# The seven-product tail of an attention and mixing kernel: its two accumulation banks made tiles of their own, its sums and splits put elsewhere

## The chip, the cores and the metric

The kernel runs on one core of a Trainium2 chip. The metric is the device time of one execution in microseconds (us). The engines are TensorE (PE, matrix products; PEld loads its weights), VectorE (DVE), ScalarE (ACT), GpSimd (POOL) and SyncE (SP, which here only starts transfers). Each works through its own list of instructions in order and waits for the others by semaphores. SBUF is the on-chip memory; PSUM holds what PE accumulates, in banks of 512 float32 columns.

## The reference

Three steps follow one another on tensors of 4 batches, 448 tokens and 768 channels.

```python
# 1  attention, 12 heads of 64
scores = scale * q @ k.T - log(448);  x = sigmoid(scores) @ v
# 2  first mixer
u = x + (x.T @ U @ V).T
x = u + relu(u @ w_ch1) @ w_ch2
# 3  second mixer
theta = x @ w_theta
y = w_tok_r @ (x * cos(theta)) + w_tok_i @ (x * sin(theta))     # over the tokens
u = x + y
out = u + relu(u @ w_ch)                                       # 768 x 768
```

The change touches the end of step 3: the token mixing of the last batch and the product with `w_ch`.

## The kernel before

**Numbers.** A float32 operand is split in a high part (ACT copies it to the matmul's format) and a low part (the operand minus the high part, by DVE, `lo_dve`, or POOL, `lo_pool`). A product is three matmuls: high x high, high x low, low x high.

**Layout.** `X` holds u with the 768 channels in 6 blocks of 128 partitions (`NK`) and the 4 x 448 tokens in its columns. `mix(b)` mixes batch b over the tokens: for each of the 6 column blocks d it runs 21 matmuls of 448 columns into one bank (`y`, two banks in turn from `ps_e`), and DVE's add then puts the result into `X` (L1078). After each add `mix` calls a hook, so what the hook emits stands on DVE, ACT and POOL between one add and the next. A bank is free for block d + 2 only when the add of block d is done.

**The seven products.** The last product is done for two batches at a time (`pr` 0 and 1, a "pair"). Of each batch 384 columns (`HN`) form the blocks of a 2 x 2 matrix: A11, A12 are the first batch's, A21, A22 the second's, by halves of the channels. A scheme of Winograd's kind takes 7 block products in place of 8. Its left operands are a11, a12, a22 and the sums s1 = a21 + a22, s3 = a11 - a21, s2 = s1 - a11 and s4 = a12 - s2 (three blocks `kk` each); its right operands b11, b21, b12, b22 and t1 to t4 were made earlier. `sums13` and `sums24` make the sums, `split_op` splits an operand into a high and a low tile.

`seven(pr, e)` does one of three output blocks: seven products of 9 matmuls of 384 columns. It uses three accumulators. b has a bank from `ps_e`; a and d are the two halves, one bank each, of one tile `ad` from `ps_t` (three such tiles of two banks). The order is a11 into a, a12 into b, s2 added into a, s1 into d, s3 added into a, s4 added into d, a22 added into a. Between them ACT copies a (p1), a again (u2) and d (p5) to SBUF, and DVE forms c11 = b + p1, c22 = a + p5, c12 = d + u2. `put` adds relu of a result to `X`, transposes it in 32 x 32 squares into a buffer `o` (a ring of five), and `store` sends it out in four transfers on SP, for the last block on SP and ACT in turn. Waits are set per tile: whoever wants to write a tile waits for the last reader of any part of it.

**The middle columns.** The 4 x 64 columns outside the two pairs (`middle`) are multiplied plainly between the pairs: 6 blocks of 18 matmuls of 256 columns, two blocks to a `wm` tile, each followed on DVE by relu-and-add (`cm`) and a transposition (`om`, in the same ring of five), stored by four transfers on SP and two each on ACT or POOL.

**Order.** The program is under a manual schedule: on each engine instructions stand as the Python emits them. Before the last `mix(3)` come the splits of a11 and all twelve sums of the first pair (they need only batches 0 and 1). In `mix(3)`'s hook, `early`, stand the splits of a12 and s2; the other splits (s1, s3, s4, a22) follow it on DVE and POOL. Then the pool of the sums, `sm`, is closed, and pool `fin` (copies, `o`, `om`, b12) takes memory that lies over it and over the mixing's weights. The hook of `seven(0, e)`, `first`, emits the splits of the middle columns and the sums of the second pair (on POOL); the second pair's s3, s4 and a22 are split after the middle columns and before `seven(1, 0)`.

**Transfers.** SP and ACT share eight counters (`DMAHW0` to `DMAHW7`), handed to their transfers in turn. A transfer waits until the one before it on its counter has landed, whichever of the two engines issued that.

Of the kernel before, what the change touches and what calls it, by code (L numbers as in the profile page):

```python
# [11 lines left out]
F32 = mybir.dt.float32  # L12
# [7 lines left out]
def f(t):  # L20
    return t.bitcast(F32)
# [3 lines left out]
def tile_kernel(  # L25
# [15 lines left out]
    nc = tc.nc  # L41
# [4 lines left out]
    P = 128  # L46
# [8 lines left out]
    HN = DM // 2  # L55
# [48 lines left out]
    def pool(name, side="left", space=None):  # L104
        st = ExitStack()
        kw = dict(name=name, bufs=1, side=side, reuse_waits="tile")
        if space is not None:
            kw["space"] = space
        return st.enter_context(tc.tile_pool(**kw)), st


    def hi_act(o, i):
        nc.scalar.activation(o, i, AF.Copy)  # L113

    def sub_pool(o, a, b):
        nc.gpsimd.tensor_sub(o, a, b)  # L116

    def lo_pool(o, i, h):
        sub_pool(o, i, f(h))

    def lo_dve(o, i, h):
        nc.vector.tensor_sub(o, i, f(h))
# [125 lines left out]
    NH3 = NK // 2  # L248
# [140 lines left out]
    def half(p, h):  # L389
        o = (h + p) % 2 * REM  # L390
        return slice(o, o + REM)
# [215 lines left out]
    for i in range(NB):  # L607
# [10 lines left out]
        if i == 0:  # L618
            name = ("w2", 1, 0)
# [316 lines left out]
    ps_t, st = pool("ps_t", "left", PSUM)  # L936
# [163 lines left out]
    for d in range(NK):  # L1100
        t = zp.tile([P, 2, HN], F32, tag="zh", name=f"stg_{NG}_{d}", bufs=12).rearrange("p a n -> p (a n)")
# [65 lines left out]
    for name, part, o in (("t3", 1, 2), ("b22", 0, 3), ("t4", 1, 3)):  # L1167
        for kk in range(NH3):
            tag, home, n = next(homes)
            load_ops(home.tile([P, 2, HN], F32R, tag=tag, name=f"{name}_{kk}", bufs=n), kk, part, o, name)  # L1170
    sm, sm_st = pool("sm", "right")

    rows_out = out.rearrange("b s d -> (b s) d")
    O, A, sums = {}, {}, {}
# [5 lines left out]
    def middle(d):  # L1180
        return X[:, d].rearrange("p (r c) -> p r c", r=B // 2)[:, :, HN:2 * S - HN]

    def op_tile(name, dtype=F32R):
        O[name] = zp.tile([P, 2, HN], dtype, tag=("zh", "zl")[len(O) % 2], name=f"op_{len(O)}", bufs=12)
        return O[name]

    def split_op(pr, name, kk, lo):
        t = op_tile((pr, name, kk))
        if name[0] == "a":
            x = half(pr, int(name[1]) - 1, (int(name[2]) - 1) * NH3 + kk)  # L1190
        elif name == "s2":
            x = O["u", pr, kk // 2][:, kk % 2]
        else:
            x = sums.pop((pr, name, kk))
        hi_act(t[:, 0], x)
        lo(t[:, 1], x, t[:, 0])
        A[pr, name, kk] = t[:, 0], t[:, 1]

    def split_ops(pr, name, *los):
        for kk in range(NH3):  # L1200
            split_op(pr, name, kk, los[kk % len(los)])

    def sum_tile(p, pr, name, kk):
        sums[pr, name, kk] = p.tile([P, HN], F32, tag="s", name=f"{name}_{pr}_{kk}", bufs=9)
        return sums[pr, name, kk]

    def sums13(p, eng, pr, kk):
        a11, a21, a22 = half(pr, 0, kk), half(pr, 1, kk), half(pr, 1, NH3 + kk)
        eng.tensor_add(sum_tile(p, pr, "s1", kk), a21, a22)
        eng.tensor_sub(sum_tile(p, pr, "s3", kk), a11, a21)  # L1210

    def sums24(p, eng, pr, kk):
        t = (O["u", pr, kk // 2] if kk % 2 else op_tile(("u", pr, kk // 2), F32))[:, kk % 2]
        eng.tensor_sub(t, sums[pr, "s1", kk], half(pr, 0, kk))
        eng.tensor_sub(sum_tile(p, pr, "s4", kk), half(pr, 0, NH3 + kk), t)

    def product(o, pr, a, b, e, start=True):
        sl = slice(e * P, (e + 1) * P)
# [26 lines left out]
        return fin.tile([P, HN], F32, tag="c", name=name, bufs=5)  # L1245

    def seven(pr, e, after):
        th = ps_t.tile([P, 2, 512], F32, tag="th", name=f"ad_{pr}_{e}", bufs=3)
        a, d = th[:, 0, :HN], th[:, 1, :HN]
        b = ps_e.tile([P, 512], F32, tag="y", name=f"b_{pr}_{e}", bufs=2)[:, :HN]  # L1250

        def copy(x, name):
            t = temp(f"{name}_{pr}_{e}")
            nc.scalar.copy(t, x)
            return t

        def both(x, t):
            nc.vector.tensor_add(t, x, t)
            return t
        product(a, pr, "a11", "b11", e)  # L1260
        p1 = copy(a, "p1")
        after(0)
        product(b, pr, "a12", "b21", e)
        after(1)
        c11 = both(b, p1)
        product(a, pr, "s2", "t2", e, False)
        u2 = copy(a, "u2")
        put(pr, 0, 0, e, c11)
        after(2)
        product(d, pr, "s1", "t1", e)  # L1270
        p5 = copy(d, "p5")
        after(3)
        product(a, pr, "s3", "t3", e, False)
        c22 = both(a, p5)
        after(4)
        product(d, pr, "s4", "b22", e, False)
        c12 = both(d, u2)
        put(pr, 1, 1, e, c22)
        after(5)
        product(a, pr, "a22", "t4", e, False)  # L1280
        put(pr, 0, 1, e, c12)
        put(pr, 1, 0, e, a)
        after(6)

    def early(d):
        if d == 0:
            split_ops(0, "a12", lo_pool)
        elif d < NH3 + 1:
            split_op(0, "s2", d - 1, lo_dve)
        elif d == NH3 + 1:  # L1290
            split_op(0, "s1", 0, lo_dve)

    split_ops(0, "a11", lo_pool)
    for kk in range(NH3):
        sums13(sm, nc.vector, 0, kk)
    for kk in range(NH3):
        sums24(sm, nc.vector, 0, kk)
    mix(3, early)
    split_op(0, "s1", 1, lo_dve)
    split_op(0, "s1", 2, lo_pool)  # L1300
    split_ops(0, "s3", lo_dve, lo_dve, lo_pool)
    split_ops(0, "s4", lo_dve, lo_dve, lo_pool)
    split_ops(0, "a22", lo_pool, lo_dve)
    sm_st.close()
    tokhl_st.close()
    fin, fin_st = pool("fin", "right")
    ctx.enter_context(fin_st)
# [4 lines left out]
    def split_m(d):  # L1312
        t = op_tile(("m", d))
        us_t[d] = t[:, 0, :2 * P], t[:, 1, :2 * P]
        h, l = (x.rearrange("p (r c) -> p r c", r=B // 2) for x in us_t[d])
        hi_act(h, middle(d))
        lo_pool(l, middle(d), h)

    def first(e):
        def after(n):  # L1320
            if e == 0 and n == 2:
                split_m(0)
            if e == 1 and n < NH3:
                sums13(fin, nc.gpsimd, 1, n)
            if e == 2 and n == 0:
                for d in range(1, 4):
                    split_m(d)
            if e == 2 and n == 1:
                for d in range(4, NK):
                    split_m(d)  # L1330
            if e == 2 and n == 2:
                split_ops(1, "a11", lo_pool)
            if e == 2 and n == 3:
                split_ops(1, "a12", lo_pool)
        return after

# [2 lines left out]
    for e2 in range(NK // 2):  # L1339
        ps = ps_t.tile([P, 2, 512], F32, tag="th", name=f"wm_{e2}", bufs=3)  # L1340
        for e in range(2):
            m = 2 * e2 + e
            n, em = divmod(m, NH3)
            o = ps[:, e, :2 * P]
            sl = slice(em * P, (em + 1) * P)
            for d in range(NK):
                wh, wl = (w[:, sl] for w in W[f"b{d // NH3 + 1}{n + 1}", d % NH3])
                xh, xl = us_t[d]
                nc.tensor.matmul(o, wh, xh, start=d == 0, stop=False)
                nc.tensor.matmul(o, wh, xl, start=False, stop=False)  # L1350
                nc.tensor.matmul(o, wl, xh, start=False, stop=d == NK - 1)
            if m < NH3:
                sums24(fin, nc.vector, 1, m)
            if m == NH3 - 1:
                split_ops(1, "s2", lo_pool)
                split_ops(1, "s1", lo_pool)
            t = temp(f"cm_{m}")[:, :2 * P]
            t3 = t.rearrange("p (r c) -> p r c", r=B // 2)
            ps3 = o.rearrange("p (r c) -> p r c", r=B // 2)
            nc.vector.scalar_tensor_tensor(out=t3, in0=ps3, scalar=0.0, in1=middle(m), op0=ALU.max, op1=ALU.add)  # L1360
            ot = fin.tile([P, HN], F32, tag="o", name=f"om_{m}", bufs=5)[:, :2 * P]
            nc.vector.transpose(out=ot, in_=t)
            for a in range(P // R):
                for k in range(REM // R):
                    (nc.sync, (nc.gpsimd, nc.scalar)[a % 2])[k].dma_start(
                        out=out[:, HN + k * R:HN + (k + 1) * R, m * P + a * R:m * P + (a + 1) * R].rearrange("n i j -> i n j"),
                        in_=ot[a * R:(a + 1) * R].rearrange("i (n k j) -> i n k j", j=R, n=B)[:, :, k],
                    )
    split_ops(1, "s3", lo_pool, lo_dve)
    split_ops(1, "s4", lo_pool, lo_dve)  # L1370
    split_ops(1, "a22", lo_pool, lo_dve)
    for e in range(NH3):
        seven(1, e, lambda n: None)


_INS = [
# [28 lines left out]
```

## Time and profile before

| | us |
|---|---|
| median of 3 runs | 1163.86 (1162.99 to 1163.92) |
| the profiled execution | 1163.92 |
| its span in the trace | 1162.1 |

The span runs from the first to the last instruction; the profiled execution's own time is 1.8 us longer. PE is busy 97% of the span, DVE 62%, ACT 32%, POOL 25%. The tail in question begins at about 1009 us with the last mixing. PE's first product of the first pair begins at 1041.6 us; the six calls of `seven` end with PE's last matmul at about 1154.6 us, with the middle columns at 1092.5 to 1107.7 us; the rest is the last stores.

In a profile row, "idle before <- releaser" is how long the engine stood still before that instruction and whose work ended that wait; line numbers are those of the kernel before.

### The profile page before, as it was taken

How to read it: one execution, taken by the hardware profiler on the slowest of the kernel's cores; microseconds unless marked ns; L12 is line 12 of the kernel's file. 1: busy time of each engine (PE TensorE's matmuls, PEld its weight loads, DVE VectorE, ACT ScalarE, POOL GpSimd, SP SyncE). 2: the span in 40 equal slices, each digit the busy share in tenths (PEclk: the TensorE clock that was granted, in tenths of full speed). 3: DMA queues.
4: the chain of work that ended last, by engine and by line, in shares of the span. 5: the costliest groups of instructions: out<-in, count | busy, mean ns of one | idle time of the engine just before them, and what ended most of it. 6: DMA issues, size and time to landing. Idle time of an engine off the chain costs nothing.

```text
span 1162.1 us, 16102 instructions
## 1 busy us (share of the span) xinstructions
PE 1125.7 (97%) x6363; PEld 935.9 (81%) x6363; DVE 716.9 (62%) x902; ACT 377.1 (32%) x511; POOL 294.3 (25%) x270
## 2 busy tenths in 40 slices
PE   9999999999999999999999999999999999988876
PEld 5554578888888888888888888888899999977765
DVE  6788685655656565657575857574667438443553
ACT  6887743222222222222222322220144426221220
POOL 6511115211211121113121412121223314422540
PEclk9999999999999999999999999999999999987999
DMA  9887302213413341335243524242483204503332
GB/s 188 167 174 147 99 28 82 82 55 87 129 55 98 86 129 55 98 98 157 77 136 109 183 89 149 97 127 82 164 267 62 36 14 120 193 1 75 53 55 51
DMA packets 231690, 120.66 MB, mean 104 GB/s; under 512 B 184448, under 2 KB 220544, under 8 KB 231488
## 3 DMA queue, kind: packets, MB, share of 16 engines
q1 hardware_dynamic: 218064, 99.58, 32.4%
q0 software_dynamic: 6768, 19.24, 5.2%
q10 hardware_dynamic: 6784, 0.82, 0.4%
q8 instruction: 50, 0.82, 0.3%
q14 instruction: 24, 0.20, 0.1%
HBM read 91.23 MB, written 28.38 MB: 103 GB/s over the span
## 4 chain that ended last, share of the span: by engine, by line
PE 93%; DVE 4%; ACT 1%; DMA 1%; issue 1%; SPq 0%; ACTq 0%; DVEq 0%
PE g L782 10%; PE y L806 10%; PE g L784 10%; PE g L783 10%; PE y L808 10%; PE y L807 10%; PE av L493 5%; PE sc L459 4%; PE y L1072 3%; PE y L1070 3%; PE y L1071 3%; PE th L956 3%; PE th L960 3%; PE th L957 3%; PE ad L1223 2%; PE ad L1225 1%
## 5 line engine op out<-in xcount | busy, mean ns | idle before, releaser
L810 DVE TENSOR_TENSOR X<-y,X 128x1024 f32<-128x1024 f32 (+1 forms) x144 | 156.6, 1088 | 232.5 <-PE y L808 232.1
L806 PE MATMUL y<-gh,w 128*128 128x512 f32 (+1 forms) x576 | 209.5, 364 | 0.6 <-DVE X L810 0.6
L782 PE MATMUL g<-uh,w 128*128 128x512 f32 (+1 forms) x576 | 209.4, 364 | 0.0
L783 PE MATMUL g<-ul,w 128*128 128x512 f32 (+1 forms) x576 | 209.3, 363 | 0.0
L807 PE MATMUL y<-gl,w 128*128 128x512 f32 (+1 forms) x576 | 209.3, 363 | 0.0
L808 PE MATMUL y<-gh,w 128*128 128x512 f32 (+1 forms) x576 | 209.2, 363 | 0.0
L784 PE MATMUL g<-uh,w 128*128 128x512 f32 (+1 forms) x576 | 209.1, 363 | 0.0
L116 POOL TENSOR_TENSOR w<-ca_w,w 128x768 fp32r<-128x768 f32 x44 | 82.5, 1874 | 390.7 <-ACT w L113 390.7
L789 ACT ACTIVATE gh<-g 128x1024 fp32r<-128x1024 f32 (+1 forms) x48 | 44.2, 920 | 341.1 <-PE g L784 341.1
L782 PEld LDWEIGHTS g<-uh,w 128*128 128x128 f32 x576 | 108.8, 189 | 17.9 <-issue 1.0
L806 PEld LDWEIGHTS y<-gh,w 128*128 128x128 f32 x576 | 108.8, 189 | 17.8 <-DVE X L810 1.0
L783 PEld LDWEIGHTS g<-ul,w 128*128 128x128 f32 x576 | 108.8, 189 | 16.9
L807 PEld LDWEIGHTS y<-gl,w 128*128 128x128 f32 x576 | 108.8, 189 | 16.9
L784 PEld LDWEIGHTS g<-uh,w 128*128 128x128 f32 x576 | 108.8, 189 | 16.8
L808 PEld LDWEIGHTS y<-gh,w 128*128 128x128 f32 x576 | 108.8, 189 | 16.8
L441 ACT ACTIVATE A<-sc,bias_s 128x896 f32<-128x896 f32 x72 | 70.0, 1014 | 12.2 <-PE sc L459 12.2
L1070 PE MATMUL y<-tok,zh 128*128 128x448 f32 x168 | 62.0, 369 | 4.0 <-DVE X L1078 4.0
L116 POOL TENSOR_TENSOR zl<-t,zh 128x768 fp32r<-128x768 f32 x21 | 39.6, 1907 | 95.7 <-ACT zh L113 70.4
L1072 PE MATMUL y<-tok,zl 128*128 128x448 f32 x168 | 62.0, 369 | 0.0
L1071 PE MATMUL y<-tok,zh 128*128 128x448 f32 x168 | 61.7, 367 | 0.0
L113 ACT ACTIVATE w<-ca_w 128x768 fp32r<-128x768 f32 x48 | 40.4, 842 | 60.8 <-PE y L808 32.2
L493 PE MATMUL av<-A,v 128*64 128x448 f32 x288 | 59.4, 548 | 0.7 <-ACT A L441 0.7
(200 smaller groups left out, 1825.1 us busy)
## 6 DMA issues: line engine op xcount, KB each, us to landing
ws_w<-in_moe_w_ch_dram SPq DMA_DIRECT2D x41, 768.0 KB, 4.4
wc_d<-sp_wc SPq DMA_DIRECT2D x12, 768.0 KB, 6.7
ws_w<-in_moe_w_ch_dram POOLq DMA_DIRECT2D x7, 768.0 KB, 6.8
q<-in_q_dram SPq DMA_DIRECT2D x90, 56.0 KB, 3.3
xn<-x_d SPq DMA_DIRECT2D x52, 96.0 KB, 2.9
k<-in_k_dram SPq DMA_DIRECT2D x86, 56.0 KB, 3.3
v<-in_v_dram POOLq DMA_DIRECT2D x12, 384.0 KB, 4.8
ws_th<-in_moe_w_theta_dram SPq DMA_DIRECT2D x6, 768.0 KB, 4.3
```

Of the source, the lines that this page charges most:

```text
L116: nc.gpsimd.tensor_sub(o, a, b)
L493: nc.tensor.matmul(ps[h * D:(h + 1) * D, :S], v_t[p // 2][:, 2 * (p % 2) + h, c, :], A_t[p, c][:, h, :], start=c == 0, stop=False,)
L782: nc.tensor.matmul(o, wh[:, sl], uh_t[g][:, kk, :], start=kk == 0, stop=False)
L783: nc.tensor.matmul(o, wh[:, sl], ul_t[g][:, kk, :], start=False, stop=False)
L784: nc.tensor.matmul(o, wl[:, sl], uh_t[g][:, kk, :], start=False, stop=kk == NK - 1)
L806: nc.tensor.matmul(o, wh[:, sl], gh[:, j, :], start=j == 0, stop=False)
L807: nc.tensor.matmul(o, wh[:, sl], gl[:, j, :], start=False, stop=False)
L808: nc.tensor.matmul(o, wl[:, sl], gh[:, j, :], start=False, stop=j == FB - 1)
L810: nc.vector.tensor_add(x, ps, x)
L1070: nc.tensor.matmul(o, zh[:, sl], tok_h[:, i, :], start=first and n == 0, stop=False)
L1071: nc.tensor.matmul(o, zh[:, sl], tok_l[:, i, :], start=False, stop=False)
L1072: nc.tensor.matmul(o, zl[:, sl], tok_h[:, i, :], start=False, stop=last and n == len(slots) - 1)
```

## The change

- `seven`: a and d are no longer halves of one tile, but each takes a tile of two banks and uses its first bank; there are still three such tiles.
- First pair: sums and splits are no longer ahead of `mix(3)`. `early` spreads the twelve sums over the hooks of column blocks 0 to 2, and the splits of a11, a12 and two of s2 over those of blocks 3 to 5. The rest of s2 and s1 follow `mix(3)`. s3, s4 and a22 are split inside the first block, behind products a11 and s1 (`late_ops`). All their low parts are DVE's.
- `sm` stays open, on the other side of the memory; `fin` now lies over the mixing's weights alone.
- Second pair: s1 and s3 are summed by DVE within `seven(0, 1)` and `seven(0, 2)`, where POOL did it within `seven(0, 1)`; s3, s4 and a22 are split inside its first block; of POOL's splits a11 and a12 remain.
- Middle columns: the splits' low parts go from POOL to DVE, and both blocks of a `wm` tile are multiplied before DVE reads either.

```diff
-    sm, sm_st = pool("sm", "right")
+    sm, sm_st = pool("sm")
+    ctx.enter_context(sm_st)
...
-        th = ps_t.tile([P, 2, 512], F32, tag="th", name=f"ad_{pr}_{e}", bufs=3)
-        a, d = th[:, 0, :HN], th[:, 1, :HN]
+        a, d = (ps_t.tile([P, 2, 512], F32, tag="th", name=f"{x}_{pr}_{e}", bufs=3)[:, 0, :HN] for x in "ad")
...
     def early(d):
-        if d == 0:
-            split_ops(0, "a12", lo_pool)
-        elif d < NH3 + 1:
-            split_op(0, "s2", d - 1, lo_dve)
-        elif d == NH3 + 1:
-            split_op(0, "s1", 0, lo_dve)
-
-    split_ops(0, "a11", lo_pool)
-    for kk in range(NH3):
-        sums13(sm, nc.vector, 0, kk)
-    for kk in range(NH3):
-        sums24(sm, nc.vector, 0, kk)
+        if d < 2:
+            for kk in ((0, 1), (2,))[d]:
+                sum1(0, kk)
+                sum3(0, kk)
+            if d:
+                sums24(0, 0)
+        elif d == 2:
+            for kk in range(1, NH3):
+                sums24(0, kk)
+        elif d < 5:
+            split_ops(0, f"a1{d - 2}", lo_dve)
+        else:
+            split_op(0, "s2", 0, lo_dve)
+            split_op(0, "s2", 1, lo_dve)
     mix(3, early)
-    split_op(0, "s1", 1, lo_dve)
-    split_op(0, "s1", 2, lo_pool)
-    split_ops(0, "s3", lo_dve, lo_dve, lo_pool)
-    split_ops(0, "s4", lo_dve, lo_dve, lo_pool)
-    split_ops(0, "a22", lo_pool, lo_dve)
-    sm_st.close()
+    split_op(0, "s2", 2, lo_dve)
+    split_ops(0, "s1", lo_dve)
...
+    def late_ops(pr, n):
+        for k, name in ((0, "s3"), (1, "s4"), (3, "a22")):
+            if n == k:
+                split_ops(pr, name, lo_dve)
     def first(e):
         def after(n):
-            if e == 0 and n == 2:
-                split_m(0)
-            if e == 1 and n < NH3:
-                sums13(fin, nc.gpsimd, 1, n)
+            if e == 0:
+                late_ops(0, n)
+                if n == 5:
+                    split_m(0)
+            if e == 1 and n < 6 and n % 2 == 0:
+                sum1(1, n // 2)
+            if e == 2 and n < 6 and n % 2:
+                sum3(1, n // 2)
...
-            if m < NH3:
-                sums24(fin, nc.vector, 1, m)
-            if m == NH3 - 1:
-                split_ops(1, "s2", lo_pool)
-                split_ops(1, "s1", lo_pool)
+        if e2 == 0:
+            sums24(1, 0)
+        elif e2 == 1:
+            sums24(1, 1)
+            sums24(1, 2)
+            split_ops(1, "s2", lo_dve)
+        else:
+            split_ops(1, "s1", lo_dve)
...
-    split_ops(1, "s3", lo_pool, lo_dve)
-    split_ops(1, "s4", lo_pool, lo_dve)
-    split_ops(1, "a22", lo_pool, lo_dve)
     for e in range(NH3):
-        seven(1, e, lambda n: None)
+        seven(1, e, lambda n: e or late_ops(1, n))
```

The first place is DVE around the first adds of `mix(3)`: L1078 are the adds (`y2_3_0` is block 0, two rows to a block), `s1_0_0` is block 0 of the first pair's s1, `op` a tile for s2. Before (six more rows of L1209 and L1210, s1 and s3, stand ahead of these):

```order
L1214 TENSOR_TENSOR op_3_8445<-s1_0_0_8433,X_63 128x384
L1215 TENSOR_TENSOR s4_0_0_8447<-X_63,op_3_8445 128x384
L1214 TENSOR_TENSOR op_3_8445<-s1_0_1_8437,X_63 128x384
L1215 TENSOR_TENSOR s4_0_1_8450<-X_63,op_3_8445 128x384
L1214 TENSOR_TENSOR op_4_8452<-s1_0_2_8441,X_63 128x384
L1215 TENSOR_TENSOR s4_0_2_8454<-X_63,op_4_8452 128x384
L1078 TENSOR_TENSOR X_63<-y2_3_0_8456,X_63 128x64
L1078 TENSOR_TENSOR X_63<-y2_3_0_8456,X_63 128x384
L1078 TENSOR_TENSOR X_63<-y2_3_1_8489,X_63 128x64
L1078 TENSOR_TENSOR X_63<-y2_3_1_8489,X_63 128x384
```

After:

```order
L1078 TENSOR_TENSOR X_63<-y2_3_0_8424,X_63 128x64
L1078 TENSOR_TENSOR X_63<-y2_3_0_8424,X_63 128x384
L1209 TENSOR_TENSOR s1_0_0_8448<-X_63 128x384
L1212 TENSOR_TENSOR s3_0_0_8450<-X_63 128x384
L1209 TENSOR_TENSOR s1_0_1_8452<-X_63 128x384
L1212 TENSOR_TENSOR s3_0_1_8454<-X_63 128x384
L1078 TENSOR_TENSOR X_63<-y2_3_1_8456,X_63 128x64
L1078 TENSOR_TENSOR X_63<-y2_3_1_8456,X_63 128x384
L1209 TENSOR_TENSOR s1_0_2_8480<-X_63 128x384
L1212 TENSOR_TENSOR s3_0_2_8482<-X_63 128x384
L1216 TENSOR_TENSOR op_0_8484<-s1_0_0_8448,X_63 128x384
L1217 TENSOR_TENSOR s4_0_0_8486<-X_63,op_0_8484 128x384
```

All twelve sums stood ahead of block 0's add; now that add comes first, and four sums stand behind each of blocks 0, 1 and 2.

The second place is PE in `seven(0, 1)`, where product s2 ends and s1 begins. Before:

```order
L1224 MATMUL ad_0_1_8770<-op_10_8567,wc_1_2_8246 128x384
L1225 MATMUL ad_0_1_8770<-op_10_8567,wc_1_2_8246 128x384
L1223 MATMUL ad_0_1_8770<-op_11_8594,wc_1_0_8242 128x384 [waits Activation_49]
L1224 MATMUL ad_0_1_8770<-op_11_8594,wc_1_0_8242 128x384
L1225 MATMUL ad_0_1_8770<-op_11_8594,wc_1_0_8242 128x384
```

After:

```order
L1226 MATMUL a_0_1_8770<-op_10_8615,wc_1_2_8246 128x384
L1227 MATMUL a_0_1_8770<-op_10_8615,wc_1_2_8246 128x384
L1225 MATMUL d_0_1_8771<-op_11_8618,wc_1_0_8242 128x384 [waits DVE_49]
L1226 MATMUL d_0_1_8771<-op_11_8618,wc_1_0_8242 128x384
L1227 MATMUL d_0_1_8771<-op_11_8618,wc_1_0_8242 128x384
```

The wait for ACT's copy u2 is gone from s1; what it waits for now is DVE's last read of the tile's former use, a of `seven(0, 0)`.

The third place is the end of SP's list, the stores of `seven(1, 1)` and `seven(1, 2)` (`o_1_1_1` is the last of the former), with the counter that each waits for. Before:

```order
L1229 DMA out_0_dram<-o_1_1_1_9456 32x12x32 [waits DMAHW4_49,DVE_49]
L1229 DMA out_0_dram<-o_1_1_1_9456 32x12x32 [waits DMAHW6_49]
L1229 DMA out_0_dram<-o_1_1_1_9456 32x12x32 [waits DMAHW0_49]
L1229 DMA out_0_dram<-o_1_1_1_9456 32x12x32 [waits DMAHW2_49]
L1229 DMA out_0_dram<-o_1_0_2_9497 32x12x32 [waits DMAHW4_49,DVE_49]
L1229 DMA out_0_dram<-o_1_0_2_9497 32x12x32 [waits DMAHW6_49]
L1229 DMA out_0_dram<-o_1_1_5_9535 32x12x32 [waits DMAHW7_49,DVE_49]
L1229 DMA out_0_dram<-o_1_1_5_9535 32x12x32 [waits DMAHW0_49]
```

After:

```order
L1231 DMA out_0_dram<-o_1_0_4_9453 32x12x32 [waits DMAHW0_49,DVE_49]
L1231 DMA out_0_dram<-o_1_0_4_9453 32x12x32 [waits DMAHW2_49]
L1231 DMA out_0_dram<-o_1_0_4_9453 32x12x32 [waits DMAHW4_49]
L1231 DMA out_0_dram<-o_1_0_4_9453 32x12x32 [waits DMAHW6_49]
L1231 DMA out_0_dram<-o_1_1_1_9460 32x12x32 [waits DMAHW7_49,DVE_49]
L1231 DMA out_0_dram<-o_1_1_1_9460 32x12x32 [waits DMAHW0_49]
L1231 DMA out_0_dram<-o_1_1_1_9460 32x12x32 [waits DMAHW2_49]
L1231 DMA out_0_dram<-o_1_1_1_9460 32x12x32 [waits DMAHW4_49]
L1231 DMA out_0_dram<-o_1_0_2_9502 32x12x32 [waits DMAHW5_49,DVE_49]
```

And ACT's transfers of the last block after the change:

```order
L1231 DMA out_0_dram<-o_1_0_2_9502 32x12x32 [waits DMAHW7_49,DVE_49]
L1231 DMA out_0_dram<-o_1_0_2_9502 32x12x32 [waits DMAHW1_49]
L1255 COPY p5_1_2_9517<-d_1_2_9467 128x384 [waits PE_49]
L1231 DMA out_0_dram<-o_1_1_5_9540 32x12x32 [waits DMAHW7_49,DVE_49]
L1231 DMA out_0_dram<-o_1_1_5_9540 32x12x32 [waits DMAHW1_49]
```

The counters were handed out in another order. Before, SP's first store of `o_1_1_5` took counter 7 behind ACT's first store of `o_1_0_5`, and 6 of SP's transfers stand from there on. Now SP's first store of `o_1_1_1` takes counter 7 behind ACT's first store of `o_1_1_5`, and 12 of SP's transfers stand from there on.

## Rows read from the trace of the kernel before

**Rows 1.** Page, busy time of each engine over the span, share, instructions.

```profile
PE 1125.7 (97%) x6363; PEld 935.9 (81%) x6363; DVE 716.9 (62%) x902; ACT 377.1 (32%) x511; POOL 294.3 (25%) x270
```

**Rows 2.** Busy time by stage: us, PE, PEld, DVE, ACT, POOL, PEclk, DMA share, GB/s.

```profile
1041.60:1063.40 21.80, 17.20 (x64) 14.85 (x64) 10.47 (x17) 3.46 (x9) 10.35 (x11) 0.69 0.24 64
1063.40:1078.00 14.60, 12.10 (x65) 10.81 (x64) 5.90 (x12) 1.44 (x3) 0.00 (x0) 1.00 0.32 54
...
1092.50:1107.70 15.20, 13.61 (x109) 13.00 (x108) 8.58 (x19) 2.60 (x6) 9.37 (x13) 1.00 0.37 63
1107.70:1125.60 17.90, 12.39 (x66) 10.80 (x65) 12.40 (x14) 5.15 (x12) 8.76 (x12) 1.00 0.21 36
```

**Rows 3.** Waits from 960 us on: total us, times, longest us.

```profile
PE ad L1223 <- ACT p L1254: 8.5, 8, 3.0
...
PE ad L1223 <- DVE p L1258: 4.3, 6, 0.7
...
PE ad L1223 <- DVE u L1258: 3.9, 6, 0.7
PE ad L1223 <- ACT u L1254: 3.4, 6, 0.6
...
PE wm L1349 <- DVE cm L1360: 1.6, 3, 0.6
```

**Rows 4.** Timeline, PE, first and last matmul of an unhindered product: start, us.

```profile
1066.41 0.33 PE L1223 MATMUL ad<-op,wc 128*128 128x384 f32 x1
...
1067.80 0.34 PE L1225 MATMUL ad<-op,wc 128*128 128x384 f32 x1
```

**Rows 5.** Timeline of the last mixing's first two blocks, POOL, DVE and PE.

```profile
1009.55 7.87 POOL L116 TENSOR_TENSOR op<-X,op 128x384 fp32r<-128x384 f32 x6
1009.88 0.62 DVE L1078 TENSOR_TENSOR X<-y,X 128x448 f32<-128x448 f32 x1 [3.58 <-PE y L1072]
...
1011.30 1.37 DVE L1209 TENSOR_TENSOR s<-X 128x384 f32<-128x384 f32 x1
...
1017.76 0.55 DVE L1210 TENSOR_TENSOR s<-X 128x384 f32<-128x384 f32 x1
...
1021.41 1.27 DVE L1078 TENSOR_TENSOR X<-y,X 128x64 f32<-128x64 f32 x4
...
1022.23 0.71 PE L1070 MATMUL y<-tok,zh 128*128 128x448 f32 x1 [3.99 <-DVE X L1078]
```

**Rows 6.** Busy time at half clock within the first call, columns as rows 2.

```profile
1058.00:1060.00 2.00, 2.00 (x7) 2.00 (x7) 0.00 (x0) 0.00 (x0) 0.00 (x0) 0.50 0.03 8
```

**Rows 7.** Timeline, where the first call of each pair waits, PE, DVE and ACT.

```profile
1046.79 0.45 PE L1223 MATMUL ad<-op,wc 128*128 128x384 f32 x1 [2.09 <-ACT p L1254]
...
1110.73 6.63 DVE L122 TENSOR_TENSOR op<-s,op 128x384 fp32r<-128x384 f32 x2 [1.92 <-ACT op L113]
...
1113.49 0.46 ACT L1254 COPY p<-ad 128x384 f32<-128x384 f32 x1
1114.00 0.45 PE L1223 MATMUL ad<-op,wc 128*128 128x384 f32 x1 [3.00 <-ACT p L1254]
```

**Rows 8.** Groups of DVE from 1092 to 1112 us: busy us, mean ns.

```profile
L1362 DVE STREAM_TRANSPOSE om<-cm 128x256 f32<-128x256 f32 x6 | 2.7, 445 | 0.2
```

**Rows 9.** Transfers from 1045 us on: issuing queue, count, size, median us to landing.

```profile
out_dram<-om SPq DMA_DIRECT2D x24, 16.0 KB, 1.5
out_dram<-o ACTq DMA_DIRECT2D x8, 48.0 KB, 1.7
out_dram<-om ACTq DMA_DIRECT2D x12, 16.0 KB, 1.6
```

**Rows 10.** Timeline, stores issued by ACT and SP: start, us, count.

```profile
1108.85 0.81 ACTq L1365 DMA_DIRECT2D out_dram<-om  x2
...
1154.05 2.95 ACTq L1229 DMA_DIRECT2D out_dram<-o  x6
...
1156.79 2.92 SPq L1229 DMA_DIRECT2D out_dram<-o  x6
```

More of the change, by code (lines that the diff above doesn't have):

```diff
@@ L1201, in split_ops, with sum_tile, sum1, sum3 @@
             split_op(pr, name, kk, los[kk % len(los)])
-    def sum_tile(p, pr, name, kk):
-        sums[pr, name, kk] = p.tile([P, HN], F32, tag="s", name=f"{name}_{pr}_{kk}", bufs=9)
+    def sum_tile(pr, name, kk):
+        sums[pr, name, kk] = sm.tile([P, HN], F32, tag="s", name=f"{name}_{pr}_{kk}", bufs=9)
         return sums[pr, name, kk]
[L1207 to L1212, printed above, removed]
+    def sum1(pr, kk):
+        nc.vector.tensor_add(sum_tile(pr, "s1", kk), half(pr, 1, kk), half(pr, 1, NH3 + kk))
+    def sum3(pr, kk):
+        nc.vector.tensor_sub(sum_tile(pr, "s3", kk), half(pr, 0, kk), half(pr, 1, kk))
+    def sums24(pr, kk):
         t = (O["u", pr, kk // 2] if kk % 2 else op_tile(("u", pr, kk // 2), F32))[:, kk % 2]
-        eng.tensor_sub(t, sums[pr, "s1", kk], half(pr, 0, kk))
-        eng.tensor_sub(sum_tile(p, pr, "s4", kk), half(pr, 0, NH3 + kk), t)
+        nc.vector.tensor_sub(t, sums[pr, "s1", kk], half(pr, 0, kk))
+        nc.vector.tensor_sub(sum_tile(pr, "s4", kk), half(pr, 0, NH3 + kk), t)
     def product(o, pr, a, b, e, start=True):
@@ L1316, in split_m @@
         hi_act(h, middle(d))
-        lo_pool(l, middle(d), h)
+        lo_dve(l, middle(d), h)
+    def late_ops(pr, n):
+        for k, name in ((0, "s3"), (1, "s4"), (3, "a22")):
+            if n == k:
+                split_ops(pr, name, lo_dve)
     def first(e):
         def after(n):
-            if e == 0 and n == 2:
-                split_m(0)
-            if e == 1 and n < NH3:
-                sums13(fin, nc.gpsimd, 1, n)
+            if e == 0:
[6 more added lines that the diff above has]
+                sum3(1, n // 2)
             if e == 2 and n == 0:
@@ L1332, in after @@
                 split_ops(1, "a11", lo_pool)
-            if e == 2 and n == 3:
+            if e == 2 and n == 4:
                 split_ops(1, "a12", lo_pool)
@@ L1341, in tile_kernel @@
         for e in range(2):
-            m = 2 * e2 + e
-            n, em = divmod(m, NH3)
+            n, em = divmod(2 * e2 + e, NH3)
             o = ps[:, e, :2 * P]
@@ L1351, in tile_kernel @@
                 nc.tensor.matmul(o, wl, xh, start=False, stop=d == NK - 1)
-            if m < NH3:
-                sums24(fin, nc.vector, 1, m)
-            if m == NH3 - 1:
-                split_ops(1, "s2", lo_pool)
-                split_ops(1, "s1", lo_pool)
+        if e2 == 0:
[6 more added lines that the diff above has]
+            split_ops(1, "s1", lo_dve)
+        for e in range(2):
+            m = 2 * e2 + e
+            o = ps[:, e, :2 * P]
             t = temp(f"cm_{m}")[:, :2 * P]
```

## Prediction

> **What bounds the kernel now.** I read the page's busy times first, then the tail by stages, then the waits, then the timelines. PE is busy 97% of the span [rows 1], so time is to be had where PE stands still or runs slowly, and the stages show where: a call of `seven` is the same work each time, yet the first takes 21.8 us at a mean granted clock of 0.69, the fourth 17.9, and the others 14.6 at full clock [rows 2]; three of the six repeat that row to 0.1. The waits say who holds PE: copies p and u by ACT and the sums by DVE, 26 waits and 20.1 us, of which 2.09 and 3.00 us are two long ones [rows 3, 7]. The remaining 24, four to a call, last 15.0 us, 0.63 each.
>
> An unhindered product has its matmuls (1067.80 - 1066.41) / 8 = 0.174 us apart [rows 4], so 63 of them need 10.9 us. A call of 14.6 thus loses 3.65 to four waits, 0.91 each: 1.46 times the idle shown, since the array also has to fill again.
>
> **The change part by part**, made against the profiled execution (1163.92; its span is 1162.1; the median of the runs, 1163.86, is the same to 0.06).
>
> *Sums within the last mixing.* DVE's twelve sums stood ahead of the first add: the first began at 1011.30, and the adds came at 1021.41; both banks were full and PE stood 3.99 us, then restarted at half clock [rows 5]. Now an add comes first, then four sums. A block of mixing lasts 0.62 + 3.58 = 4.2 us [rows 5]; add and four sums take 0.64 + 4 x 0.55 = 2.8 at the price of a sum that had POOL silent, or 0.64 + 4 x 1.37 = 6.1 at the price beside POOL [rows 5]. I take 0.55: the a11 and a12 splits that kept POOL busy are DVE's now and stand behind blocks 3 and 4 (three of 0.55 each, also below 4.2). Six blocks from 1009.9 then end at 1035.1 in place of 1041.6: **-6.5**. At 1.37 three blocks would each be 1.9 longer, leaving -0.8.
>
> *First call, `seven(0, 0)`.* Its 21.8 us hold four waits on the shared tile, the 2.09 us wait for p1 (held back until DVE had finished all splits and so freed the memory of `fin`) and half clock behind it. `fin` no longer lies over the sums, and p1 stands ahead of the s3, s4 and a22 splits. New on the path is DVE: behind the mixing's last add it has 6 low parts of s2 and s1, 6 of s3 and s4, three instructions for c11 and its store, 3 low parts of a22, and c22, 19 at about 0.5 plus the add, done some 10.0 us after the mixing. Product a22 needs c22 out of its bank and is due after six products, 9.4 us. So 0.6 of waiting, 0.9 with the refill: 21.8 to 11.8, **-10.0**. Queued behind those DVE instructions is the last put only; the next call's d, which takes over the bank of a, starts three products (4.7 us) later.
>
> *Calls two and three.* The first use of s2 on a waits for p1, s3 for u2, s4 for p5, a22 for c22, and in each case a whole other product (1.57 us) now lies between, against 0.46 for a copy or 0.55 for a sum. Nothing shows: 2 x -3.65 = **-7.3**. DVE gains three sums in each and five low parts of the middle columns in the third, which fit: its 5.9 us [rows 2] grow to some 10 of 10.9.
>
> *POOL beside DVE.* In the third call POOL splits a11 and a12 of the second pair while two of DVE's sums come due. A subtraction of DVE took 0.55 alone and 1.37 beside POOL [rows 5], and two at 1110.73 took 6.63, 3.3 each [rows 7]; sums and puts that read PSUM or are of another form kept their length. So DVE is late by 0 to 5.5; I take 2 x 0.8, the price of the same sums, of which the slack ahead of c22 takes over half: **+0.7**. The Trainium skill (GPSIMD Engine Reference, Specifications) has GpSimd share its SBUF interfaces with VectorE and names instructions with two SBUF inputs as those that suffer. The trace agrees (1.37 against 0.55). By that rule the moves of low parts from POOL to DVE help twice, and these two sums are what speaks against the change.
>
> *Middle columns.* Three waits of PE for DVE inside a `wm` tile, 1.6 us idle [rows 3], go, since both blocks are multiplied first: 1.6 x 1.46 = **-2.3**, 15.2 to 12.9.
>
> *Fourth call, `seven(1, 0)`.* p1 stood behind nine high parts on ACT (3.00 us of waiting [rows 7]). It now stands ahead of them, but behind ACT's last `om` stores, and DVE's `om` buffers are a ring of five with o's: the sixth takes the first one's buffer, whose SP stores wait, by the shared counters, for ACT's stores of the third. From the start of the middle columns: DVE's backlog, two sums, then cm and om of the first tile by 6.4, four sums and three low parts by 10.0, third om 10.9, ACT's two stores 0.81 [rows 10], 1.6 to landing [rows 9], SP's four stores about 1.7, 1.5 to landing [rows 9], so the sixth om starts near 16.5 and ends 0.45 later [rows 8], two stores 0.8, p1 0.46 [rows 7]: about 18.4. Product s2 is due two products behind the middle columns, 12.9 + 3.1 = 16.0. So 2.5 us of waiting and 0.3 of refill remain; a22 is late by 0.5 as in the first call. 17.9 to 14.2, **-3.7**. Without the ring's wait it would be -6.5, with the old 3.00 -3.2.
>
> *Calls five and six.* -3.65, and three waits' worth in the last, -2.75, since behind its s4 the end is DVE's chain of puts, which has the same length as before: **-6.4**.
>
> *The last stores.* SP's last 6 transfers began at 1156.79, 2.92 us for six, after a landing of ACT's store [rows 10]. In the new order 12 of them wait for the first landing of ACT's `o_1_1_5` store, issued as the one at 1154.05 was [rows 10], plus 1.7 [rows 9]: 1.0 earlier, but six more at 0.5. **+2.0**, at worst; 0 if the order is not kept by such waits.
>
> Sum: -6.5 - 10.0 - 7.3 + 0.7 - 2.3 - 3.7 - 6.4 + 2.0 = **-33.5**, so 1163.92 - 33.5 = **1130.4**. With every remaining wait and the tail's extra at zero it would be 6.9 less, 1123.5; slow ends below.
>
> **Rivals.**
>
> *The clock falls at a wait that is left.* A wait of 2.09 us was followed by half clock, the 3.00 us one was not: its stage has 1.00 [rows 2, 7]. The remaining 2.5 us wait may go either way. In the first call 0.69 over 21.8 us means 13.5 us at half clock, where 7 matmuls took 2.0 us [rows 6], 0.29 against 0.174 each: 13.5 x 0.4 = 5.4, giving 1135.8; a short fall as in the mixing (6.5 - 4.0 = 2.5) gives 1132.9. The Trainium skill (TensorE: Matmul & The Clock Gate, What's actually happening) has the gate watch activity free of the kernel's start, so the same wait can fall either way in different runs; the two waits here agree with that, and it is why this is a chance and not a term.
>
> *DVE becomes the bound.* It takes over all low parts and reaches 10 of 10.9 us in a call. If c22 comes late by a wait's worth in every call, 6 x 0.91 = 5.5: 1135.9. For it: a22's 0.6 in the first call; against: calls two, five and six have no splits.
>
> *The waits don't go.* If PE still meets a reader of the other bank at each product, the 22 us of four waits per call stay, less what the copy's new place gives: 1130.4 + 20 = 1150. Against: the order of PE shows the wait for ACT gone.
>
> *Slower: the clock stays low.* If a wait early in the tail brings half clock and the smaller waits keep it there through all six calls, 378 matmuls at 0.29 - 0.174 = 0.116 more cost 44: 1174. It decides from 33.5 / 0.116 = 290 matmuls on. For it: the first call stayed at half clock for 13.5 us; against: calls with four waits of 0.63 each ran at 1.00 [rows 2], and there will be fewer.
>
> **How the numbers follow.** Forecast 62% (its own range 1126 to 1134); the clock 21%; DVE 10%; waits that stay 4%; slower 2%; the rest beyond. Range: 1124, the end without leftovers, to 1139, both 5.5 us rivals partly together; left out are 4 and 2% and a share of the tails. This kernel's runs tell 0.2%, 2.3 us, from no change; every case but the last is faster by more: faster 96%, same 2%, slower 2%.
>
> **What would show it.** Right: PE without idle from about 1010 to 1035 and clock 1.00 there; calls two, three, five at 10.9; no wait of PE's products for a copy u; a wait of 2 to 3 us before the second pair's s2; 12 SP stores behind ACT's in the tail. Wrong: blocks of mixing longer than 4.2, calls at 14.6, DVE's sums beside POOL at 3 us with PE waiting for c22, or PEclk of 0.5 in any stage.

## Result and profile after the change

The changed kernel takes 1130.88 us (median of 4 runs, 1129.78 to 1131.10) against 1163.89 of the kernel before (4 runs, 1162.99 to 1172.03): 33.0 us less, a ratio of the medians of 0.9716. The ratio over all runs is 0.9699, with a 95% interval of 0.9656 to 0.9743; it lies lower because one of the four runs before took 1172.03. Its profiled execution took 1130.86 us with a span of 1128.8.

The page's busy times, to be held against [rows 1]:

```profile
PE 1112.1 (99%) x6363; PEld 932.0 (83%) x6363; DVE 721.2 (64%) x937; ACT 377.4 (33%) x511; POOL 259.8 (23%) x235
```

PE has the same 6363 matmuls; DVE gained 35 instructions and POOL lost as many: the low parts and sums that changed engines. The stages, as in [rows 2]: us, then PE, PEld, DVE, ACT, POOL busy, PEclk, DMA share, GB/s.

```profile
1046.80:1057.70 10.90, 10.90 (x64) 10.90 (x64) 7.05 (x14) 1.44 (x3) 0.00 (x0) 1.00 0.43 72
1057.70:1068.60 10.90, 10.90 (x66) 10.90 (x65) 8.82 (x19) 5.37 (x14) 5.18 (x5) 1.00 0.44 75
1068.60:1081.50 12.90, 12.90 (x110) 12.90 (x109) 11.22 (x23) 1.37 (x4) 5.78 (x10) 1.00 0.37 63
1081.50:1096.70 15.20, 13.06 (x65) 12.52 (x64) 11.15 (x24) 6.52 (x15) 2.47 (x5) 0.89 0.32 51
1096.70:1107.60 10.90, 10.90 (x65) 10.90 (x64) 5.68 (x11) 1.44 (x3) 0.00 (x0) 1.00 0.43 74
```

These are calls two and three, the middle columns, and calls four and five. Where a call lasted 14.6 with PE busy 12.1, it lasts 10.90 with PE busy throughout. Of these calls only the fourth is longer, at a mean clock of 0.89. All waits of PE from 960 us on: total us, times, longest us.

```profile
PE a L1225 <- ACT p L1255: 2.1, 1, 2.1
PE a L1225 <- issue: 0.6, 1, 0.6
```

Of the 26 waits at `ad` of [rows 3] one is left, and one is new; the waits at `wm`, and the one in the last mixing, are gone. The new one stands in the first call at 1044.97 (0.58 us): product a22, behind DVE's addition of c22, which ended at 1044.87.

### The profile page after: what moved, and what is told of

Read it like the earlier page. It is cut to its first block, busy times and chain, and to the rows that moved or that the text cites. A ratio compares the mean times of both kernels' runs of the same rounds, so it can differ in the third digit from the quotient of the medians.

```text
span 1128.8 us, 16091 instructions
## 1 busy us (share of the span) xinstructions
PE 1112.1 (99%) x6363; PEld 932.0 (83%) x6363; DVE 721.2 (64%) x937; ACT 377.4 (33%) x511; POOL 259.8 (23%) x235
## 4 chain that ended last, share of the span: by engine, by line
PE 95%; DVE 2%; DMA 1%; issue 0%; ACT 0%; ACTq 0%; SPq 0%; DVEq 0%
PE g L782 10%; PE y L806 10%; PE g L784 10%; PE g L783 10%; PE y L808 10%; PE y L807 10%; PE av L493 5%; PE sc L459 4%; PE y L1072 3%; PE y L1070 3%; PE y L1071 3%; PE th L956 3%; PE th L957 3%; PE th L960 3%; PE a L1225 1%; PE a L1227 1%
```

## Experiments

Each ratio below is to the kernel before as it ran beside that experiment, with its 95% interval; differences in us are to 1163.89, or to the 1130.88 of the changed kernel. The kernel before took 1164.21 to 1165.15 us beside the experiments, so differences of about 1 us between kernels that did not run beside each other are not told apart.

**The two halves of the change alone.** e1_banks_only is the kernel before with a and d as tiles of their own. The second kernel is the changed one with a and d as halves of one tile again.

```diff
 e1_banks_only, against the kernel before
-        th = ps_t.tile([P, 2, 512], F32, tag="th", name=f"ad_{pr}_{e}", bufs=3)
-        a, d = th[:, 0, :HN], th[:, 1, :HN]
+        a, d = (ps_t.tile([P, 2, 512], F32, tag="th", name=f"{x}_{pr}_{e}", bufs=3)[:, 0, :HN] for x in "ad")
 e2_order_only, against the changed kernel: the same lines, the other way round
```

> The kernel before with one edit: a and d of the seven products are tiles of their own. Theory (each PE wait for a reader of the other half costs 0.91 us, and nothing else holds the products of calls two, three, five and six): those four calls fall from 14.6 to 10.9, the last by three waits only, 13.7 us together; the first and fourth call lose their four waits too but keep the long wait for p1: 2 to 7 us more in all. Time 1143 to 1149, last mixing still with its 4 us of idle PE. Rival (the order is what counts; behind each removed wait stands DVE or ACT with late splits): 1158 or more.

> The kernel after with a and d again halves of one tile; order, pools and splits as changed. Theory: the four waits come back in every call, 3.65 each and 2.75 in the last: 21 us, less what they hide of the 2.1 us wait and the low clock in the fourth call: 1148 to 1152. Rival (the order is what counts): at most 5 us above 1130.9, so below 1136.

The banks alone: 1143.85 us (1140.52 to 1144.64), ratio 0.9819 [0.98, 0.9838], 20.0 less than before. The order alone: 1148.02 (1147.43 to 1153.45), 0.9871 [0.9845, 0.9896], 15.9 less than before. Both are as the theory had it. In e1 the second call has PE busy for all of its 10.92 us:

```profile
1057.19:1068.11 10.92, 10.92 (x65) 10.92 (x64) 6.45 (x13) 1.44 (x4) 0.00 (x0) 1.00 0.43 74
```

The waits that are left in e1 lie elsewhere: one in the last mixing, those for p1 in the first call of each pair, and three in the middle columns, of which one is longer than before (2.00 us, where the longest was 0.6):

```profile
1022.09 0.45 PE L1070 MATMUL y<-tok,zh 128*128 128x448 f32 x1 [3.98 <-DVE X L1078]
1045.95 0.44 PE L1223 MATMUL a<-op,wc 128*128 128x384 f32 x1 [2.08 <-ACT p L1253]
...
1081.58 0.38 PE L1348 MATMUL wm<-op,wc 128*128 128x256 f32 x1 [2.00 <-DVE cm L1359]
...
1100.47 0.44 PE L1223 MATMUL a<-op,wc 128*128 128x384 f32 x1 [3.17 <-ACT p L1253]
```

In e2 the second call has the four waits back, and lasts 14.58 us:

```profile
1054.55 0.45 PE L1225 MATMUL ad<-op,wc 128*128 128x384 f32 x1 [0.57 <-ACT u L1256]
1056.96 0.45 PE L1225 MATMUL ad<-op,t 128*128 128x384 f32 x1 [0.57 <-ACT p L1256]
1059.51 0.45 PE L1225 MATMUL ad<-op,b 128*128 128x384 f32 x1 [0.72 <-DVE p L1260]
1062.03 0.44 PE L1225 MATMUL ad<-op,t 128*128 128x384 f32 x1 [0.65 <-DVE u L1260]
```

PE waited because the bank that it was to write shared a tile with a bank that ACT or DVE was reading; nothing else in the call changed. 20.0 + 15.9 is 2.9 more than 33.0, and the traces say where the halves overlap: in the first call. From the last add of the mixing to p1 of the second call it is 23.4 us before, 16.4 in e1, 16.1 in e2 and 13.4 after the change, so each half takes off 7 or more and both together 10.1. From p1 of the third call to p1 of the fifth it is the other way: 47.7, 43.6, 45.1 and 39.0 us, so both take off 2.0 more than the two alone.

**The last mixing: the place of the sums, or POOL beside them.** The change did two things at once there: it spread the sums behind the blocks, and it took a11's and a12's low parts from POOL. Two conditions make four corners, and the changed kernel has both cures. e5_sums_ahead puts the sums ahead again, with POOL silent; e6_pool_beside has POOL's splits ahead as well, so it has neither cure, like the kernel before; e9_pool_spread has POOL's splits, with the sums spread.

```diff
 e5_sums_ahead, against the changed kernel (`early` does nothing at d < 3)
+    for kk in range(NH3):
+        sum1(0, kk)
+        sum3(0, kk)
+    for kk in range(NH3):
+        sums24(0, kk)
     mix(3, early)
 e6_pool_beside: as e5, without a11, a12 in `early`, but with these two lines ahead of the sums; e9_pool_spread: with them too, and the sums as in the changed kernel
+    for x in "12":
+        split_ops(0, f"a1{x}", lo_pool)
```

> The kernel after with the first pair's twelve sums moved back ahead of the last mixing's first add; the splits of a11 and a12 stay DVE's, so POOL is silent there. Theory C (POOL beside DVE made the sums long, and that was the 4 us wait): twelve sums at 0.5 end near 1017.5 us, the add near 1018.1, PE needs the bank at 1018.2: within 0.5 us of the kernel after, 1130.4 to 1131.4. Rival P (the place of the sums ahead of the add is the cost, as the prediction had it): the wait of some 4 us and the low clock return, 1135 to 1137.5.

> As the kernel with the sums ahead, and the splits of a11 and a12 ahead of them with POOL's low parts, as in the kernel before. Theory C: sums at 1.37 beside POOL, the wait of 4 us and low clock behind it: 1135 to 1137.5. Rival P: the same as the kernel with the sums ahead and POOL silent, to 0.5 us.

> The fourth corner of two conditions: the sums stand spread behind the blocks of the last mixing, as in the changed kernel, but POOL takes the low parts of a11 and a12 ahead of it, as in the kernel before. Theory (either cure alone is enough): POOL is busy from about 1009.6 to 1017.5; the first add comes at 1014.04, two or three sums behind it take 1.37 instead of 0.55 (issued 1.29 apart instead of 0.47), so the four end at about 14.64 + 2 x 1.29 + 2 x 0.47 = 1018.2, on time for the second add at 1018.24, and PE does not wait: 1129.5 to 1132. Rival (POOL's presence sets the cost wherever the sums stand, as the prediction's far end had it): blocks of mixing 1.9 longer, PE waits in the mixing, 1134 to 1137.

e5 took 1130.55 us (1129.88 to 1131.08), 0.9703 [0.9679, 0.9727]; e6 1136.26 (1136.11 to 1136.64), 0.9752 [0.9729, 0.9776]; e9 1130.46 (1129.83 to 1131.08), 0.9701 [0.9674, 0.9727]. Three corners are equal, and one is 5.4 to 5.8 slower. In the stage itself it is 6.4 us: the mixing's last add starts at 1041.48 in e6, at 1035.04 in the changed kernel, 1035.12 in e5 and 1035.01 in e9. Part of it comes back in the fourth call, where the clock fell in the changed kernel and in e9, but not in e6 (see the last section). DVE in the changed kernel, then in e5, e6 and e9 (start, us; the add of a block is L1078):

```profile
1014.04 0.69 DVE L1078 TENSOR_TENSOR X<-y,X 128x64 f32<-128x64 f32 x2 [2.71 <-PE y L1072]
1014.64 0.55 DVE L1209 TENSOR_TENSOR s<-X 128x384 f32<-128x384 f32 x1
...
1018.24 0.69 DVE L1078 TENSOR_TENSOR X<-y,X 128x64 f32<-128x64 f32 x2 [1.64 <-PE y L1072]
```

```profile
1011.21 0.55 DVE L1209 TENSOR_TENSOR s<-X 128x384 f32<-128x384 f32 x1
...
1017.21 0.68 DVE L1078 TENSOR_TENSOR X<-y,X 128x64 f32<-128x64 f32 x2
1018.21 0.69 DVE L1078 TENSOR_TENSOR X<-y,X 128x64 f32<-128x64 f32 x2 [0.32 <-PE y L1072]
```

```profile
1011.12 1.37 DVE L1209 TENSOR_TENSOR s<-X 128x384 f32<-128x384 f32 x1
...
1017.58 0.55 DVE L1212 TENSOR_TENSOR s<-X 128x384 f32<-128x384 f32 x1
...
1021.23 1.28 DVE L1078 TENSOR_TENSOR X<-y,X 128x64 f32<-128x64 f32 x4
```

```profile
1014.01 0.69 DVE L1078 TENSOR_TENSOR X<-y,X 128x64 f32<-128x64 f32 x2 [2.70 <-PE y L1072]
1014.61 0.90 DVE L1209 TENSOR_TENSOR s<-X 128x384 f32<-128x384 f32 x1
1015.44 1.36 DVE L1212 TENSOR_TENSOR s<-X 128x384 f32<-128x384 f32 x1
1016.72 0.55 DVE L1209 TENSOR_TENSOR s<-X 128x384 f32<-128x384 f32 x1
...
1018.21 0.69 DVE L1078 TENSOR_TENSOR X<-y,X 128x64 f32<-128x64 f32 x2 [0.47 <-PE y L1072]
```

Twelve sums ahead, 0.47 or 0.59 apart, end at 1017.2 in e5, before the second block needs its add (1018.2). In e6 five of them are 1.29 apart while POOL works; they end at 1021.2, and both banks are full. Spread, as in e9, they wait out most of POOL's work. POOL and PE in e6, then POOL in e9:

```profile
1009.37 7.87 POOL L116 TENSOR_TENSOR op<-X,op 128x384 fp32r<-128x384 f32 x6
```

```profile
1022.06 0.71 PE L1070 MATMUL y<-tok,zh 128*128 128x448 f32 x1 [3.99 <-DVE X L1078]
```

```profile
1009.48 6.91 POOL L116 TENSOR_TENSOR op<-X,op 128x384 fp32r<-128x384 f32 x6
```

Either cure alone gives all of the gain in this stage. POOL pays as well: its six splits take 7.87 us beside five long sums, 6.91 beside two.

**The splits of the first block.** e7_splits_early does those of s3, s4 and a22 ahead of the first call, instead of between its products.

```diff
     split_ops(0, "s1", lo_dve)
+    for name in ("s3", "s4", "a22"):
+        split_ops(0, name, lo_dve)
...
             if e == 0:
-                late_ops(0, n)
```

> The kernel after with the first pair's s3, s4 and a22 split before its first call, not within it. Theory (of the first call's 10 us the tiles gave 3.65 and the memory of fin the rest; the place of the splits gives nothing, since ACT's nine high parts end near 1037 and p1 is due at 1038, and the same number of DVE instructions stands ahead of c22): within 0.5 us of the kernel after. Rival (p1 behind the high parts waits as in the second pair before): 2 to 3 us of waiting, 1133 to 1136.

1130.78 us (1129.62 to 1132.17), 0.9705 [0.968, 0.973]: nothing. For the first pair the later place of these splits is worth no time that these runs can tell. e7 also bears on the 2.09 us of [rows 7]. In it p1 is copied at 1036.35, while DVE's splits, all ahead of it in the program, run on to 1042.4; in the kernel before it waited for them. So p1 no longer depends on the splits, which speaks for the place of `fin`, as predicted. That place was not changed alone, and neither were the middle columns or the second pair's sums and splits.

**What is left: the `om` stores of ACT, and the last stores.** e3_om_on_pool sends all the second halves of the `om` stores from POOL instead of from ACT and POOL in turn; e4_tail_pool does the last block's stores from SP and POOL instead of SP and ACT; e8_both_stores has both edits.

```diff
 e3_om_on_pool
-                    (nc.sync, (nc.gpsimd, nc.scalar)[a % 2])[k].dma_start(
+                    (nc.sync, nc.gpsimd)[k].dma_start(
 e4_tail_pool
-        queues = [nc.sync, nc.scalar] if (pr, e) == (B // 2 - 1, NH3 - 1) else [nc.sync]
+        queues = [nc.sync, nc.gpsimd] if (pr, e) == (B // 2 - 1, NH3 - 1) else [nc.sync]
```

> The kernel after with the middle columns' stores that ACT issued issued by POOL. Theory (the wait of 2.1 us before the second pair's s2 comes from the copy p1 standing behind ACT's om stores, which wait for buffers and counters of SP's): the wait goes, and the 3.4 us at half clock behind it: 3 to 4 us less, 1127 to 1128. Rival (DVE's own delay in the ring of five buffers or its low parts hold s2 or the product after it): within 1 us of 1130.9.

> The kernel after with the last block's stores on SP and POOL in place of SP and ACT. Theory (SP's last 12 stores stand behind the landing of ACT's store of o_1_1_5 by the shared counters): SP no longer waits for another engine's store, the end comes some 4 us earlier, 1126 to 1128. Rival (the end is the landing of the last buffer's stores, whoever issues them, or POOL issues more slowly than ACT): within 1 us of 1130.9.

> The kernel after with both edits of the stores: the middle columns' on SP and POOL, the last block's on SP and POOL. Theory (the two gains, 4.4 and 2.5 us, lie in different places): 1123.5 to 1124.5. Rival (with POOL's counters used by both, or SP's list now the end, one of the gains goes): 1126 or more.

e3 took 1126.51 us (1126.35 to 1127.05), 0.9676 [0.9662, 0.9691], 4.4 under the changed kernel. DVE and ACT in the changed kernel, where p1 of the fourth call is late:

```profile
1084.92 0.45 DVE L1376 STREAM_TRANSPOSE om<-cm 128x256 f32<-128x256 f32 x1 [0.26 <-DMA out_dram<-om]
```

```profile
1084.39 1.89 ACTq L1379 DMA_DIRECT2D out_dram<-om  x4
1086.32 0.48 ACT L1255 COPY p<-a 128x384 f32<-128x384 f32 x1 [3.48 <-DMA out_dram<-om]
```

and in e3 the same copy, with the window of the call (columns as above):

```profile
1083.14 0.48 ACT L1255 COPY p<-a 128x384 f32<-128x384 f32 x1 [4.78 <-PE a L1227]
```

```profile
1081.50:1092.70 11.20, 11.20 (x65) 10.95 (x64) 9.81 (x21) 5.18 (x12) 6.74 (x13) 1.00 0.33 57
```

The copy follows PE instead of a transfer, 3.2 us earlier, and no wait of PE is left from the second call on. The call lasts 11.20 in place of 15.20 us.

e4 took 1128.35 us (1128.18 to 1129.46), 0.9694 [0.9678, 0.971]: the right direction, 2.5 us, a little less than expected (1126 to 1128). The last stores in the changed kernel, then in e4:

```profile
1118.72 3.11 ACTq L1231 DMA_DIRECT2D out_dram<-o  x6
...
1120.40 6.02 SPq L1231 DMA_DIRECT2D out_dram<-o  x12
```

```profile
1119.22 3.65 POOL L1231 DMA_DIRECT2D out_dram<-o  x6 [4.81 <-DVE o L1242]
```

From DVE's last transpose to the end it is 8.0 us in the changed kernel, 5.3 in e4: SP no longer issues 12 in a row behind a landing of ACT's. POOL's stores, 0.61 apart, now come last.

e8 took 1123.71 us (1123.54 to 1123.76), 0.9644 [0.9616, 0.9672]: 7.2 under the changed kernel and 40.2 under the one before. It beats both.

## Why the prediction was right

The forecast of 1130.4 is 0.5 under the median, and its terms came out as follows; the working stands above.

- *Last mixing, -6.5:* blocks 4.2 us apart, the last add at 1035.04: -6.5. The size was right, and so was the price of 0.55 per sum. But the text tied it to the new order as well, and e5 shows that silence of POOL alone does it. Its far end, blocks 1.9 longer beside POOL with only 0.8 gained, was wrong: in e9 the spread order with POOL at work loses nothing, since POOL is done at 1016.4 and only two sums are long before the second add at 1018.21.
- *First call, -10.0:* the p copies of calls one and two are 1036.62 and 1048.40, so the call lasts 11.8 as forecast. The wait for c22 was put at 0.6 and was 0.58.
- *Calls two and three, -7.3:* 2 x (14.6 - 10.9) = 7.4. e1 gives this to the banks alone, e2 takes it away again. DVE was busy for 7.05 and 8.82 of the 10.90 us, less than the 10 that the text had.
- *POOL beside DVE in the third call, +0.7:* mis-sized; it cost nothing. Three DVE instructions were long, and PE did not wait for them. The text also read the 6.63 us of [rows 7] as two of 3.3 each; they are one of 6.16 and one of 0.55 (the row of before, with shortest, middle and longest in ns, stands last):

```profile
1063.98 0.88 DVE L1212 TENSOR_TENSOR s<-X 128x384 f32<-128x384 f32 x1
...
1068.68 0.75 DVE L1212 TENSOR_TENSOR s<-X 128x384 f32<-128x384 f32 x1
1069.36 1.37 DVE L1240 SCALAR_TENSOR_TENSOR X<-u,X 128x384 f32<-128x384 f32 x1
```

```profile
L122 DVE TENSOR_TENSOR op<-s,op x2: 548/3356/6164, 1110.7 to 1116.8; 128x384 fp32r<-128x384 f32 x2
```

- *Middle columns, -2.3:* 12.90 us as forecast.
- *Fourth call, -3.7:* 15.20 in place of 14.2, so -2.7. The wait for p1 was there, 2.14 us for 2.5, behind ACT's `om` stores as worked out; but the ring of buffers was hardly what held it. The ring held DVE up for 0.26 us only (the row at 1084.92 above). The chain that ended last runs through ACT's list twice: ACT's high parts of s1 stood behind its stores of the second tile, to 1081.4, and p1 behind those of the third, the last of which began at 1085.96, just after a landing:

```profile
1079.73 1.77 DMA out_dram<-om
1081.51 0.52 ACT op L113
...
1084.39 1.55 DMA out_dram<-om
...
1086.32 0.49 ACT p L1255
```

  So the size fits in part by luck, and "without the ring's wait it would be -6.5" was wrong: that wait was 0.26 us. The step that made the error in time is the clock's, which stood as a rival: here it fell behind that wait, as this window and the wait ahead of it show, and in e5, at the same place with a longer wait, it did not:

```profile
1086.85 0.44 PE L1225 MATMUL a<-op,wc 128*128 128x384 f32 x1 [2.14 <-ACT p L1255]
```

```profile
1087.00:1094.00 7.00, 7.00 (x32) 7.00 (x33) 5.71 (x12) 4.50 (x11) 0.00 (x0) 0.76 0.25 40
```

```profile
1087.11 0.44 PE L1225 MATMUL a<-op,wc 128*128 128x384 f32 x1 [2.31 <-ACT p L1255]
```

```profile
1087.00:1094.00 7.00, 6.54 (x36) 6.22 (x36) 6.35 (x14) 4.64 (x12) 0.08 (x1) 1.00 0.25 41
```

  From p1 of the fourth call to p1 of the fifth it is 12.01 us here and 10.97 in e5: the fall costs 1.0, where the rival had 2.5 for a short one and 5.4 for a long one. Without it the call would have had its 14.2. The low clock itself took more, some 1.6 us (eleven matmuls in 3.47 us, from 1087.84 to 1091.31, at 0.174 they need 1.91), but it hid the late c22, for which e5 waits 0.50 us. The rival's price was also too low: a matmul at half clock takes 0.32 us, by the starts in the first call of the kernel before (six from 1058.19 to 1059.79), and not 0.29: the 7 of [rows 6] count two that the window's edges cut. Its long fall would have been 6.2 and its slow case 55 in place of 44.
- *Calls five and six, -6.4:* from 1096.70 to the end of DVE's last transpose 24.09 us, against 1125.60 to 1156.13, 30.53, before: -6.4.
- *Last stores, +2.0:* 8.0 us behind that transpose, 6.0 before: +2.0, with 12 of SP's stores in a row. e4 shows the cause. It came with the tiles of a and d: e1, where nothing else was changed, has the 12 stores in a row and 8.0 us behind DVE's last transpose, e2 has 6 and 5.9 (rows of e1, then e2). How the tiles lead to another order of the counters stayed open.

```profile
1133.79 6.01 SPq L1229 DMA_DIRECT2D out_dram<-o  x12
```

```profile
1140.05 2.90 SPq L1231 DMA_DIRECT2D out_dram<-o  x6
```

The sum of the measured terms is -33.3 (6.5 + 10.0 + 7.4 + 2.3 + 2.7 + 6.4 - 2.0), that of the profiled executions 1163.92 - 1130.86 = 33.1. The two errors, -0.7 and +1.0, nearly cancel; that the forecast lies within 0.5 us is in part luck. DVE as the bound, waits that stay, and a clock that stays low did not occur.

## What to carry to other kernels

Banks that are written and read in turn belong in tiles of their own: one shared tile cost 0.91 us at each change of hands ([rows 2] against the call in e1), 20 us here with nothing else altered. Where an engine is late, ask first what its instructions cost when the neighbour is silent: moving POOL's work and moving the sums each gave the stage's whole 6.4 us, and together no more. A transfer's end can hold up work that has nothing to do with it, when that work stands in an engine's list behind stores that wait for landings: look for "<-DMA" ahead of a short copy, as here (4.4 us, the clock's 1.0 among them), and at the last stores (2.5 us).

## What the runs showed of the hardware

- The length of a wait alone does not decide whether the granted clock falls behind it. At the wait for p1 of the fourth call the changed kernel (2.14 us of waiting), e9 (2.32) and e4 (2.37) had a mean of 0.76 from 1087 to 1094 us, in the first with 0.50, the lower level, from 1088.6 to 1090.6. It stayed at 1.00 behind the same wait in e6 (2.14), e2 (2.28), e5 (2.31) and e7 (2.51). Behind 3.00 us in the kernel before it stayed at 1.00 [rows 2, 7]; behind 3.17 us in e1 it was 0.62 from 1100.50 to 1105.00. The changed kernel and e5 have the same one wait ahead of it in the tail, 0.58 and 0.60 us, so the waits do not tell them apart; what decides stayed open.
- A put beside POOL took 1.37 us in place of 0.52 (the row at 1069.36): the prediction had held that puts keep their length. This one reads u and X, both in SBUF, as the sums do. The Trainium skill (GPSIMD Engine Reference, Specifications) names two SBUF inputs as the case that contends. The rows agree in part: every long one shown has two such inputs, but the put at 1067.59 reads p and X, both in SBUF as well, with POOL busy throughout, and kept its 0.55. What else it takes stayed open.

```profile
1063.42 6.89 POOL L116 TENSOR_TENSOR op<-X,op 128x384 fp32r<-128x384 f32 x6 [53.87 <-ACT op L113]
...
1067.59 0.55 DVE L1240 SCALAR_TENSOR_TENSOR X<-p,X 128x384 f32<-128x384 f32 x1
```

- The same six splits of POOL took 6.91 us beside two long sums and 7.87 beside five: both engines' work gets longer.
